# Values of both head pairs in one visit, left keys in four 64x64 tiles, and softmax sums half a quad later, in a fused soft-capped attention and max-of-two MoE kernel

## The chip, the cores and the metric

The kernel runs on one core of one Trainium2 chip. The metric is the device time of one execution in microseconds (us), and each kernel is given by the median of its runs. Engines: PE is TensorE's matmul, PEld its weight load, DVE VectorE, ACT ScalarE, POOL GpSimd, SP SyncE, whose queue issues most of the transfers ("SPq"). PSUM is the memory that this kernel's matmuls write and that DVE copies out ("evacuates") before it is written again; a "ones matmul" multiplies by a matrix of ones and so adds up the sums of the softmax. The "granted clock" is the share of TensorE's full clock that the profile shows.

## The reference, cut to what matters

```python
scores = q @ k^T / sqrt(64)                    # q, k, v: 8 batches x 12 heads x 448 x 64
scores = 30 * tanh(scores / 30)
attn   = exp(scores - max) / sum(...)          # softmax over 448 keys
x      = (attn @ v), heads side by side        # 3584 x 768
h1, h2 = x @ w1, x @ w2                        # 768 -> 1024
out    = maximum(h1, h2) @ w_out               # 1024 -> 768
```

The kernel writes max(h1, h2) as h2 + relu(h1 - h2). So it needs one product with `wd = w1 - w2`, a relu, and two products into the output, with `w_out` and with `wm = w2 @ w_out`, which is multiplied out once at the start.

## The kernel before: the parts that matter

Two heads make a pair, two pairs a quad; there are 24 quads. 448 keys are three blocks of 128 (`j` below) and 64 left over. A quad's left keys of both pairs lie in one tile, `expo[t, 2]`. Six pairs make one batch of tokens, three quads, and the MoE of a batch may start only when all its x is there.

```python
def values(t, ab):                       # one pair: 6 matmuls into 64 columns each, one full one for the left keys
    ps = pv_psum.tile([P, 512], f32, name="pv")
    for j in range(NJ):
        for h in range(2):
            nc.tensor.matmul(ps[HALF[h], :S], vp[g % 2][:, 2 * n + h, j, :], e_of(t, ab, j)[:, h, :], ...)
    nc.tensor.matmul(ps[:, :S], vl[g % 2][:, n, :], expo[t, 2][:, ab, :], start=False, stop=True)

# a quad's sums, on their way to x (17 of the 24 quads):
def total(t):    # ones matmuls on esum, copy to st, then: SP queue   sums <- st        (7 KB)
def invert(t):   # DVE reciprocal of sums, then:             SP queue   DRAM <- reciprocal
def spread(t):   #                                           SP queue   rec_b <- DRAM, to all partitions
def normalize(t):# POOL: x = u * rec_b, one multiply for each pair
# the other 7 quads ("CHIP") turn the sums with DVE transposes on the core, without a transfer
```

The main loop gives every engine its order. `F(n)` puts n MoE matmuls ("fill") into PE's order; `add` are the DVE additions that make the sums. Shortened:

```python
for t in range(3, NQ):
    if t % 3 == 0 and 3 < t < 13 or ...:  fill_q.append(moe(t // 3 - 1))   # a batch's MoE may start
    scores(t + 1, 0); ex(t, 3); F(2); add(t, 0, 1); F(6)
    if t in crosses: cross(crosses[t])      # SP queue: transposing DMA of a group of keys and queries
    spread(t - 2)                           # SP queue
    extra(i); F(5)                          # loads (SP queue) and casts (POOL) of groups to come
    scores(t + 1, 1); ex(t + 1, 0)
    keep(t, 0, values(t, 0))                # first visit, DVE copies the values to u
    F(4); add(t, 1, 0); F(6)
    normalize(t - 2)                        # POOL
    scores(t + 1, 2); ex(t + 1, 1)
    add(t, 0, 2); F(2); add(t, 1, 2); F(4); add(t, 1, 1); F(2)
    invert(t - 1)                           # DVE waits here for the sums of the quad before
    extra(i + 1); F(2)
    scores(t + 1, 3); ex(t + 1, 2)
    keep(t, 1, values(t, 1)); total(t)      # second visit, then at once the sums; sums <- st leaves here
    ...
```

## Time and profile before

| | before |
|---|---|
| median (runs) | 379.11 us (378.74 to 380.28) |
| span of the profiled execution, mean granted clock | 381.4 us, 0.977 |
| ACT busy; tanh and exp, the work that only ACT has | 281.6 us |
| ACT's idle gaps between its instructions (each about 0.2 us or more), added up from the timeline | 33.3 us, of which 18.2 in the first 75 us |
| length of an undisturbed quad | 11.8 us, ACT busy 11.7 of it |
| end of ACT's last exp to the end of the span (the "tail") | 63.9 us: ACT idle, PE busy 60.2, DVE 25.5 |

The way to read it: as long as ACT has work, a microsecond in which ACT stands is a microsecond of time, and one in which another engine stands costs nothing unless it makes ACT stand. The views that carry this are shown inside the prediction.

### The profile page before, as it was taken

What the parts mean: (1) busy time and instruction counts of PE and PEld (TensorE: products, weight loads), DVE (VectorE), ACT (ScalarE), POOL (GpSimd) and SP (SyncE); (2) the same over time, 40 slices, a digit from 0 to 9 for tenths busy, and PEclk for the clock granted to TensorE, in tenths of its full rate; (3) what the DMA queues carried; (4) which work ended last, traced back from release to release, by engine and by line L of the source; (5) the groups of instructions that cost most, each with busy time, mean ns of one, the idle gap of its engine ahead of it and who ended that gap; (6) DMA issues with size and microseconds to landing.
All of it is one profiled execution on the core that took longest, in us unless ns stands there. A gap on an engine that the chain in (4) does not pass through costs nothing.

```text
span 381.4 us, 6115 instructions
## 1 busy us (share of the span) xinstructions
PE 350.7 (92%) x2278; PEld 166.6 (44%) x2278; DVE 249.9 (66%) x413; ACT 281.6 (74%) x265; POOL 159.3 (42%) x193
## 2 busy tenths in 40 slices
PE   4799998999599988899999979999999899999996
PEld 2345443444144433244443434444443345555563
DVE  4237657868667768687877785787776878433521
ACT  4993778999869997699999996999999893000000
POOL 6644693703473238413582293427744232220000
PEclk9999999999789998899999998999999999999999
DMA  7999979573966599459994976788985032332022
GB/s 258 259 221 297 327 202 258 168 199 90 270 217 151 118 274 281 70 142 257 270 259 113 267 234 163 208 257 243 188 235 165 2 92 92 104 98 103 5 83 84
DMA packets 109523, 69.80 MB, mean 183 GB/s; under 512 B 64308, under 2 KB 104500, under 8 KB 109492
## 3 DMA queue, kind: packets, MB, share of 16 engines
q1 hardware_dynamic: 107540, 66.25, 62.3%
q0 software_dynamic: 1952, 3.15, 4.4%
q8 instruction: 18, 0.29, 0.3%
q14 instruction: 13, 0.11, 0.1%
HBM read 50.27 MB, written 11.13 MB: 161 GB/s over the span
## 4 chain that ended last, share of the span: by engine, by line
PE 45%; ACT 32%; DVE 7%; issue 4%; SPq 4%; DMA 3%; POOL 3%; POOLq 0%; DVEq 0%; ACTq 0%
ACT expo L306 15%; ACT tanh L299 14%; PE mm L455 11%; PE mm L470 10%; PE mm L467 7%; PE s L298 4%; PE pv L341 3%; PE mm L235 3%; ACT tanh L301 3%; DVE esum L329 2%; DMA qr<-in_q_dram 2%; PE pv L344 2%; POOL xT L418 1%; SPq L137 1%; SPq L271 1%
## 5 line engine op out<-in xcount | busy, mean ns | idle before, releaser
L299 ACT ACTIVATE tanh<-s 128x896 bf16<-128x896 f32 x144 | 124.2, 914 | 31.3 <-PE s L298 29.6
L306 ACT ACTIVATE expo<-tanh 128x1792 bf16<-128x1792 bf16 (+1 forms) x96 | 144.8, 1509 | 0.1
L470 PE MATMUL mm<-wo_sb,gT 128*128 128x384 bf16 x448 | 88.3, 332 | 0.0
L455 PE MATMUL mm<-xT,wd_sb 128*128 128x448 bf16 x384 | 82.1, 362 | 4.4 <-POOL xT L418 2.5
L418 POOL TENSOR_TENSOR xT<-u,rec_b 128x448 bf16<-128x448 f32 x34 | 41.8, 1248 | 96.1 <-DMA rec_b<-rec_d 75.0
L467 PE MATMUL mm<-wm_sb,xT 128*128 128x384 bf16 x336 | 69.9, 331 | 3.2 <-DVE osb L474 1.8
L470 PEld LDWEIGHTS <-gT 128*128 128x128 bf16 x448 | 43.4, 99 | 32.0 <-issue 5.8
L455 PEld LDWEIGHTS <-wd_sb 128*128 128x128 bf16 x384 | 37.1, 100 | 42.8 <-issue 10.8
L298 PE MATMUL s<-qkT 64*128 64x448 bf16 x288 | 46.4, 374 | 9.9 <-ACT tanh L299 4.8
L474 DVE COPY osb<-mm 128x384 f32<-128x384 f32 x56 | 30.9, 552 | 34.6 <-PE mm L470 34.4
L459 DVE TENSOR_SCALAR gT<-mm 128x448 bf16<-128x448 f32 x64 | 39.6, 619 | 18.5 <-PE mm L455 18.3
L350 DVE COPY u<-pv 128x448 f32<-128x448 f32 x38 | 23.3, 614 | 36.1 <-PE pv L344 34.3
L467 PEld LDWEIGHTS <-xT 128*128 128x128 bf16 x336 | 32.3, 99 | 24.7 <-issue 4.7
L329 DVE TENSOR_TENSOR esum<-esum,expo 128x896 bf16<-128x896 bf16 x42 | 38.9, 927 | 2.4
L159 POOL CAST vp<-vr 128x1152 bf16<-128x1152 f32 x14 | 16.8, 1203 | 46.4 <-DMA vr<-in_v_dram 30.8
L341 PE MATMUL pv<-expo,vp 128*64 128x448 bf16 x288 | 36.2, 359 | 0.0
L325 DVE TENSOR_TENSOR esum<-esum,expo 64x896 bf16<-64x896 bf16 x42 | 32.4, 771 | 0.8
L327 DVE TENSOR_TENSOR esum<-expo 128x896 bf16<-128x896 bf16 x42 | 31.8, 758 | 0.0
L298 PEld LDWEIGHTS <-qkT 64*128 64x128 bf16 x288 | 11.8, 95 | 44.2 <-issue 41.7
L301 ACT ACTIVATE tanh<-s 128x896 bf16<-128x896 f32 x24 | 22.0, 917 | 3.7 <-PE s L293 2.9
L341 PEld LDWEIGHTS <-vp 128*64 128x64 bf16 x288 | 13.1, 109 | 17.0 <-issue 11.8
L179 POOL CAST kqf<-kr 128x1152 bf16<-128x1152 f32 x14 | 17.3, 1237 | 5.5 <-DMA kr<-in_k_dram 5.2
(74 smaller groups left out, 268.7 us busy)
## 6 DMA issues: line engine op xcount, KB each, us to landing
kr<-in_k_dram SPq DMA_DIRECT2D x14, 576.0 KB, 5.6
qr<-in_q_dram SPq DMA_DIRECT2D x14, 576.0 KB, 7.0
vr<-in_v_dram SPq DMA_DIRECT2D x14, 576.0 KB, 4.4
out_dram<-osb SPq DMA_DIRECT2D x20, 384.0 KB, 3.6
rec_b<-rec_d SPq DMA_DIRECT2D x34, 224.0 KB, 3.6
out_dram<-osb SPq DMA_DIRECT2D x16, 192.0 KB, 3.1
osb<-in_moe_w_dram SPq DMA_DIRECT2D x4, 512.0 KB
gT<-in_moe_w_dram POOLq DMA_DIRECT2D x6, 256.0 KB, 11.9
```

What stands on the lines that cost most here:

```text
L298: nc.tensor.matmul(s[:, h, :S], k0[r, j * P : (j + 1) * P], qTn[r, :])
L299: nc.scalar.activation(tanh[t, p][:, 2 * m : 2 * m + 2, :], s[:, :, :S], AF.Tanh, scale=scale / cap)
L301: nc.scalar.activation(tanh[t, p][:, 0:2, :], s[:, :, :S], AF.Tanh, scale=scale / cap)
L306: nc.scalar.activation(expo[t, p], tanh[t, p][:, 0:n, :], AF.Exp, scale=float(cap))
L325: nc.vector.tensor_add(d, d, expo[t, 2][r, :, :])
L329: nc.vector.tensor_add(d, d, e_of(t, ab, 0 if ab else 2))
L341: nc.tensor.matmul(ps[HALF[h], :S], vp[g % 2][:, 2 * n + h, j, :], e_of(t, ab, j)[:, h, :], start=(j == 0), stop=False)
L418: nc.gpsimd.tensor_mul(x_of(t, ab), U[t][:, ab, :], rec[t][:, ab, :])
L455: nc.tensor.matmul(ps[:, :S], wd_sb[:, c, f * P : (f + 1) * P], x[:, c, cs], start=(c == 0), stop=(c == KC - 1))
L459: nc.vector.tensor_relu(g[:, f, cs], ps[:, :S])
L467: nc.tensor.matmul(ps[:, : DM // 2], x[:, c, ts], wm_sb[:, c, hs], start=(c == 0), stop=False)
L470: nc.tensor.matmul(ps[:, : DM // 2], g[:, f, ts], wo_sb[:, f, hs], start=False, stop=(f == FC - 1))
```

## The change

Its intent: fewer and wider DVE operations, no full matmul for 64 left keys, and no wait of PE for the additions behind the sums. The core of the diff:

```diff
-    def values(t, ab):          # per pair, one bank
+    def values(t):              # both pairs, one PSUM tile of two banks
+        ps = pv_psum.tile([P, 2, 512], f32, name="pv")
+        ...                     # 12 matmuls of 64 columns
+        for ab in range(2):
+            for h in range(2):
+                r = HALF[h ^ ab]
+                nc.tensor.matmul(ps[HALF[h], ab, :S], vl[g % 2][r, n, :], expo[t, 2][r, ab, :], start=False, stop=True)
+        nc.vector.tensor_copy(U[t], ps[:, :, :S])                  # one copy of 896 columns
@@ casts of the left keys and values (POOL): by odd and even pair, twice as many, with half the columns
-                eng.tensor_copy(vl[g % 2][r, n0:n1, r], l[r, n0:n1, :])
+                for n, to in left_rows(g, par):
+                    eng.tensor_copy(vl[g % 2][to, n, :], l[64 * par : 64 * par + 64, n, :])
@@ the 7 CHIP quads: both pairs in one chain (ones, transpose, reciprocal, transpose), multiplied on POOL
-        nc.vector.tensor_mul(x_of(t, 1), ps[:, :S], rb)
+        normalize(t)
@@ main loop
+        if t > 4 and t - 2 not in CHIP:
+            spread(t - 2)                      # now ahead of cross
         F(6)
         if t in crosses:
             cross(crosses[t])
-        if t > 4 and t - 2 not in CHIP:
-            spread(t - 2)
         ...
         extra(i)
         scores(t + 1, 1); ex(t + 1, 0)
-        keep(t, 0, values(t, 0))
+        sums_of(t - 1)                         # total(t - 1), or the chain of a CHIP quad
         ...
         invert(t - 1)                          # where it was
         ...
         scores(t + 1, 3); ex(t + 1, 2)
-        keep(t, 1, values(t, 1)); total(t)
+        values(t)
```

In one quad, 5 (`QUICK`), the chain still follows its values at once. A quarter of the diff rewrites the first three quads, the start, in the same style.

## The prediction

> **What bounds the kernel now.** I read the page's busy shares and slices first. PE is at 92% of the span and ACT at 74%, but ACT's work lies in the first 32 of 40 slices.
>
> ```profile
> PE 350.7 (92%) x2278; PEld 166.6 (44%) x2278; DVE 249.9 (66%) x413; ACT 281.6 (74%) x265; POOL 159.3 (42%) x193
> PE   4799998999599988899999979999999899999996
> ACT  4993778999869997699999996999999893000000
> PEclk9999999999789998899999998999999999999999
> ```
>
> So there are two phases. Up to about 317 us the attention's tanh and exp run on ACT, while PE fills its free time with a fixed count of MoE matmuls per quad (two head pairs). After that PE works alone, without a gap, through what is left. The tail's work is nearly fixed, so every microsecond by which ACT's phase ends sooner moves the end by one.
>
> Second, windows of single quads, then of the bad places (columns: PE, PEld, DVE, ACT, POOL busy, granted clock, DMA share, GB/s):
>
> ```profile
> 185.26:197.08 11.82, 11.44 (x75) 5.37 (x74) 8.27 (x13) 11.69 (x12) 11.31 (x14) 1.00 0.96 257
> 197.08:208.89 11.81, 11.81 (x72) 4.96 (x71) 9.96 (x16) 11.68 (x11) 4.40 (x5) 1.00 0.59 158
> 144.00:162.00 18.00, 16.18 (x84) 6.26 (x84) 13.25 (x16) 12.41 (x13) 12.38 (x15) 0.81 0.68 165
> 225.00:236.00 11.00, 8.30 (x45) 3.24 (x46) 7.97 (x9) 7.78 (x8) 6.94 (x8) 0.84 0.59 165
> ```
>
> A good quad takes 11.81 us with ACT busy 11.68 of it: ACT bounds it, and PE has little to spare (in the quad at 185 it waited for ACT's tanh 0.23 + 0.15 us). Nothing cheaper on PE or DVE shortens such a quad. In the bad windows ACT, PE and the clock all drop. Third, therefore, the waits of ACT and PE, and the timeline around one:
>
> ```profile
> ACT tanh L299 <- PE s L298: 29.6, 16, 5.6
> PE ss L362 <- DVE esum L329: 4.5, 2, 2.7
> ...
> 225.21 4.08 DVE L329 TENSOR_TENSOR esum<-esum,expo 128x896 bf16<-128x896 bf16 x1
> 225.51 2.21 POOL L418 TENSOR_TENSOR xT<-u,rec_b 128x448 bf16<-128x448 f32 x2
> 229.35 0.37 PE L362 MATMUL ss<-esum,ones 128*32 128x448 bf16 x2 [2.69 <-DVE esum L329]
> 231.68 1.73 ACT L299 ACTIVATE tanh<-s 128x896 bf16<-128x896 f32 x2 [2.54 <-PE s L298]
> 232.50 2.25 PE L470 MATMUL mm<-wo_sb,gT 128*128 128x384 bf16 x8
> ```
>
> This is one whole event. The last add of the quad's sums meets a POOL multiply and takes 4.08 us where it takes 0.62 alone. The ones matmul on those sums follows at once in PE's order, so PE stands for 2.69 us, the next scores come late, ACT stands for 2.54 us, and eight matmuls then take 2.25 us (1.30 at full clock).
>
> Adding ACT's single gaps in the timeline: 9.1 us at 34, 40, 44 and 55 us, plus 1.55 at 62 (the start); 4.70 at 108; 0.77 + 1.49 + 2.66 + 0.63 = 5.55 from 144 to 162; 2.54 + 0.65 = 3.19 at 231 and 235; 0.30 + 0.29 + 0.57 + 0.45 = 1.6 elsewhere. All but the start comes to 15.0 us.
>
> [...] two 64-row score matmuls of 448 columns take 0.24 us start to start, two 64-column value matmuls 0.23, and the full 128x128 one 0.20. That four 64x64 matmuls of this width pass together, no line shows. [...] the trace has 614 for the copy and 638 to 645 for the transposes. [...]
>
> **The change part by part.**
>
> (1) Left keys. Two 128x128 matmuls a quad (2 x 0.20 = 0.40 us) become four 64x64 ones into two banks. Side by side, my estimate from the 0.23 pairs is 0.25 us, so 0.15 saved. The two value visits become one: [...] That is some 0.3 us of PE a quad, 7 us over 24 quads. In ACT-bound quads it is only slack. It counts in the last two, PE-bound, quads: 0.5 us.
>
> (2) Wide DVE operations. Removed: 38 copies x 0.614 + 28 transposes x 0.642 + 14 reciprocals x 0.237 + 10 multiplies x 0.62 = 23.3 + 18.0 + 3.3 + 6.2 = 50.8 us. Added: 24 copies of 896 columns; [...] 1.08 each, 25.9 us; 14 transposes at 1.11, 15.5; 7 reciprocals at 0.26, 1.8; in all 43.2. DVE saves about 7.6 us of 250, nearly all off the path.
>
> (3) POOL takes the 10 multiplies that DVE did: 10 x 1.24 = 12.4 us. Each left cast is split by odd and even pair: two 64x192 pieces at about 0.34 become four at about 0.27 (from 0.18 fixed plus 0.83 ns a column), 0.4 us each for keys and values, over 16 groups 12 us. POOL goes from 159 to about 184 us, not a bound, but these sit in its order.
>
> (4) Sums half a quad later. The ones matmuls of quad t come after the second scores of t+1, some 5 us after the last add. A 4 us add ends before them. That removes the stalls at 152 and 226 us. With two reciprocal buffers, DVE's second transpose no longer waits for POOL (2.01 us at 141.7[...]).
>
> (5) Spread before cross. The broadcast of the reciprocals of quad 3 was issued at 95.50, behind a 3.28 us transposing DMA that held the queue, though they had been stored at 83.79; POOL's multiply therefore ran at 100.21 and PE's first MoE matmul of the second batch waited 1.60 us. Now it goes first. But quad 5 (done at once, "QUICK") has the chain copy 1.08, ones 0.4, transpose 1.11, reciprocal 0.25, transpose 1.11, POOL 2 x 1.24, some 6.5 us after its values, with about 3 us of other PE work over it. Before, the stall ended 6.7 us after the values. I keep a stall of 3 us, and take 1.5 us off.
>
> **The sum.** Start +0.5; stall at 100 to 108 -1.5; 144 to 162 -4.5 of 5.55; 231 to 235 -2.9 of 3.19; small gaps -1.0 of 1.6; last quads -0.5; new waits on the one two-bank value tile and on copies behind a long add +1.5. Together -8.4 us, or 370.7; I say 370.5.
>
> The start is my least sure term. In it PE is the bound, and 16 fewer fill matmuls (about 2.6 us) are asked of it before quad 3; but quad 0's sums now wait for the 1.08 us copy out of the same PSUM tile. Worse, the first three quads are normalized on POOL: the multiply of quad 1 stands ahead of four 2.13 us subtractions and the casts of group 3, and that of quad 2 behind them. I get quad 2 ready at about 60 to 63 us, against a MoE start that waited until 60.69 before.
>
> **The rivals.** (a) PE is the hidden bound everywhere, and its saving comes in full: 7 us more, 363 to 365. For it speaks PE's 11.81 of 11.81 in one quad; against it, ACT's 11.68 of the same quad and PE's waits for tanh. (b) The four small matmuls do not overlap: 4 x 0.19 = 0.76 us instead of 0.40, +0.36 a quad against a measured slack of 0.38. Quads would become PE-bound and much of the gain go, 373 to 377. [...] (c) POOL's larger load stretches DVE's adds more often (they already average 927, 771 and 758 ns against 0.62), or holds the first normalizations; stalls then come back at the PSUM evacuations or near 60 us: 374 to 379. POOL's idle 58% speaks against it, its place in the order for it. (d) The long value burst, [...] 3.3 us between scores, starves ACT: ACT then has 1.6 + 1.73 + 0.85 = 4.2 us queued, so no, by 0.7 us.
>
> **Range and chances.** The removed stalls are seen in the trace and the cure is direct, so slower is unlikely. The 2% line is 371.5, just above my figure. Range 364.5 to 376.5. Faster by over 2%: 0.57; within 2%: 0.39; slower: 0.04.
>
> **What would show it.** Right: no wait of the ones matmuls on the sums; quads still 11.8 us with ACT at 11.7; ACT's gaps after 100 us down from 15.0 to about 5; the four 64x64 matmuls in about 0.25 us; ACT's last exp 7 to 9 us sooner and the tail as long as before. Wrong: quads shorter than 11.8 us or PE the longer in them (then a); 0.6 us or more for the four (b); PE waiting for POOL's xT near 60 or 100 us longer than before, or for osb and gT copies (c); regular small ACT gaps after the values (d).

## The result, and the profile after

The changed kernel takes 408.27 us (median of 4 runs, 405.48 to 409.02) against 379.69 us of the kernel before in the same rounds. The ratio is 1.073, with a 95% interval from 1.067 to 1.080. (A ratio is the mean time of one kernel's fast runs over that of the other's of the same rounds, so it is not quite the ratio of the medians quoted.) It is clearly slower, by 28 us.

The page after, to be held against the page lines in the prediction (busy us, share, instructions; then 40 slices):

```profile
PE 351.5 (86%) x2326; PEld 166.9 (41%) x2326; DVE 250.2 (61%) x369; ACT 281.7 (69%) x265; POOL 188.9 (46%) x265
PE   3689996999599958599969997795999999999996
ACT  4795665999769986489967999983999996000000
PEclk9999997999989998799997999996999999999999
```

PE, DVE and ACT do as much work as before, to within 1 us. Only POOL does more, about as foreseen. What has changed is that PE and ACT now have dents together at slices 11, 15 to 17, 21 and 28, and that ACT's last quad comes 25 us later. The chain that ended last says of what kind the dents are. First before, then after:

```profile
PE 45%; ACT 32%; DVE 7%; issue 4%; SPq 4%; DMA 3%; POOL 3%; POOLq 0%; DVEq 0%; ACTq 0%
```

```profile
PE 38%; ACT 17%; POOL 12%; DMA 11%; SPq 9%; DVE 7%; issue 5%; POOLq 0%; DVEq 0%; ACTq 0%
```

Transfers and the SP queue went from 7% to 20% of the span, POOL from 3% to 12%. The path that sets the end now runs through a transfer again and again. The longest waits after (engine, line, what it waited for: us in all, times, the longest):

```profile
ACT tanh L311 <- PE s L310: 48.6, 20, 7.0
...
DVE rec_s L406 <- DMA sums<-st: 39.4, 11, 8.3
...
PE mm L445 <- POOL xT L428: 12.5, 8, 3.5
```

The second line is new. DVE's reciprocal of the sums waits for the transfer of the sums. What sat before that instruction, by the view of the tile `sums`, in before and after:

```profile
  DMA sums<-st: 1.3, 1
```

```profile
  DMA sums<-st: 39.4, 11
```

One of the eleven, in order of time. Before, around 127 us (start, duration, engine, line, operation):

```profile
126.87 0.61 DVE L366 COPY st<-ss 128x448 f32<-128x448 f32 x1
...
127.51 0.61 SPq L368 DMA_DIRECT2D sums<-st  x1
...
129.51 3.42 SPq L271 DMA_TRANSPOSE qkT<-kqf  x1
...
136.11 0.48 DVE L396 RECIPROCAL rec_s<-sums 32x56 f32<-32x56 f32 x1
```

The sums leave 0.03 us after their copy, and the reciprocal is asked for 8.6 us later: no wait. After, the same piece of another quad:

```profile
138.33 5.64 SPq L283 DMA_TRANSPOSE qkT<-kqf  x1
...
138.70 0.62 DVE L374 COPY st<-pv 128x448 f32<-128x448 f32 x1 [0.73 <-PE pv L372]
...
144.66 1.28 SPq L143 DMA_DIRECT2D kr<-in_k_dram  x2
...
147.33 0.62 SPq L376 DMA_DIRECT2D sums<-st  x1
...
151.34 0.49 DVE L406 RECIPROCAL rec_s<-sums 32x56 f32<-32x56 f32 x1 [8.33 <-DMA sums<-st]
151.76 1.01 DVE L366 COPY u<-pv 128x896 f32<-128x896 f32 x1
...
153.82 0.32 PE L457 MATMUL mm<-wm_sb,xT 128*128 128x384 bf16 x1 [4.31 <-DVE osb L464]
...
154.70 1.73 ACT L311 ACTIVATE tanh<-s 128x896 bf16<-128x896 f32 x2 [3.48 <-PE s L310]
```

The copy is done at 139.32, half a quad later than it would have been before. But it is now behind a transposing DMA and loads in the SP queue, so its transfer leaves only at 147.33, 8.0 us later, and its data is there at 151.3. DVE has stood 8.33 us by then, with the copy of the values and the evacuation of MoE results behind the reciprocal in its order. PE finds no free PSUM and stands 4.31 us, the next scores are late, ACT stands 3.48 us. The two windows on either side (us; PE, PEld, DVE, ACT, POOL busy; clock) show what it costs. The first quad is still the 11.8 us one, although DVE stands in it, and the bill comes in the second:

```profile
139.44:151.22 11.78, 9.16 (x61) 4.43 (x60) 3.05 (x5) 11.68 (x11) 2.22 (x2) 1.00 1.11 230
151.22:168.60 17.38, 11.14 (x65) 4.58 (x65) 14.91 (x16) 11.68 (x11) 11.64 (x17) 0.88 0.57 179
```

A second kind of dent lies where a batch's MoE starts. At 212 us, around the start of the fourth batch:

```profile
200.44 1.14 POOL L166 CAST vp<-vr 128x1152 bf16<-128x1152 f32 x1 [11.26 <-DMA vr<-in_v_dram]
201.53 1.95 POOL L171 CAST vl<-vr 64x64 bf16<-64x64 f32 x4
...
204.91 1.57 POOL L203 CAST kqf<-kr 64x128 bf16<-64x128 f32 x4
...
208.62 4.64 POOL L428 TENSOR_TENSOR xT<-u,rec_b 128x448 bf16<-128x448 f32 x4
...
212.22 0.53 PE L445 MATMUL mm<-xT,wd_sb 128*128 128x448 bf16 x1 [3.51 <-POOL xT L428]
...
214.80 1.73 ACT L311 ACTIVATE tanh<-s 128x896 bf16<-128x896 f32 x2 [4.50 <-PE s L310]
```

POOL's order has a value cast, whose load was late, then casts of a whole group, then four multiplies in a row that make the batch's last x. PE comes to that x at 208.7 and stands 3.51 us, ACT 4.50.

Adding up all of ACT's gaps of about 0.2 us or more gives 58.5 us after and 33.3 before. The difference is 25.2 us of the 25.8 by which the spans differ (407.2 and 381.4): 6.1 in the first 75 us, 19.1 later. So the whole loss is ACT standing, and three suspects are left: the round trip of the sums, x late at batch starts, and the start.

### The profile page after: what moved, and what is told of

It is laid out like the page before. It is cut to its first block, busy times and chain, and to the rows that moved or that the text cites. A ratio compares the mean times of both kernels' runs of the same rounds, so it can differ in the third digit from the quotient of the medians.

```text
span 407.2 us, 6229 instructions
## 1 busy us (share of the span) xinstructions
PE 351.5 (86%) x2326; PEld 166.9 (41%) x2326; DVE 250.2 (61%) x369; ACT 281.7 (69%) x265; POOL 188.9 (46%) x265
## 4 chain that ended last, share of the span: by engine, by line
PE 38%; ACT 17%; POOL 12%; DMA 11%; SPq 9%; DVE 7%; issue 5%; POOLq 0%; DVEq 0%; ACTq 0%
PE mm L445 13%; PE mm L460 9%; ACT expo L318 8%; ACT tanh L311 8%; PE mm L457 7%; POOL xT L428 4%; DMA sums<-st 4%; DMA qr<-in_q_dram 4%; PE s L310 4%; DMA vr<-in_v_dram 3%; PE pv L354 3%; SPq L283 3%; POOL kqf L190 3%; SPq L137 2%; POOL wd_sb L229 2%
## 5 line engine op out<-in xcount | busy, mean ns | idle before, releaser
L445 PE MATMUL mm<-xT,wd_sb 128*128 128x448 bf16 x384 | 90.4, 383 | 22.5 <-POOL xT L428 12.5
L428 POOL TENSOR_TENSOR xT<-u,rec_b 128x448 bf16<-128x448 f32 x48 | 59.8, 1269 | 64.0 <-DMA rec_b<-rec_d 46.8
L457 PE MATMUL mm<-wm_sb,xT 128*128 128x384 bf16 x336 | 68.5, 329 | 7.2 <-DVE osb L464 7.0
L445 PEld LDWEIGHTS <-wd_sb 128*128 128x128 bf16 x384 | 37.8, 103 | 68.1 <-issue 39.4
L166 POOL CAST vp<-vr 128x1152 bf16<-128x1152 f32 x14 | 16.5, 1181 | 85.1 <-DMA vr<-in_v_dram 41.3
L339 DVE TENSOR_TENSOR esum<-expo 128x896 bf16<-128x896 bf16 x42 | 37.4, 890 | 0.2
L337 DVE TENSOR_TENSOR esum<-esum,expo 64x896 bf16<-64x896 bf16 x42 | 36.6, 871 | 0.6
L366 DVE COPY u<-pv 128x896 f32<-128x896 f32 x24 | 25.6, 1067 | 14.4 <-PE pv L362 14.2
L341 DVE TENSOR_TENSOR esum<-esum,expo 128x896 bf16<-128x896 bf16 x42 | 32.2, 767 | 2.1
L354 PE MATMUL pv<-expo,vp 128*64 128x448 bf16 x288 | 31.8, 356 | 1.0 <-DVE wm_sb L580 1.0
L406 DVE RECIPROCAL rec_s<-sums 32x56 f32<-32x56 f32 x17 | 8.3, 488 | 39.4 <-DMA sums<-st 39.4
L203 POOL CAST kqf<-kr 64x128 bf16<-64x128 f32 (+1 forms) x56 | 21.6, 385 | 3.7 <-DMA kr<-in_k_dram 1.9
## 6 DMA issues: line engine op xcount, KB each, us to landing
out_dram<-osb SPq DMA_DIRECT2D x20, 384.0 KB, 3.6
```

The costliest lines, as they stand in the source:

```text
L337: nc.vector.tensor_add(d, d, expo[t, 2][r, :, :])
L339: nc.vector.tensor_add(d, e_of(t, ab, 1 if ab else 0), e_of(t, ab, 2 if ab else 1))
L341: nc.vector.tensor_add(d, d, e_of(t, ab, 0 if ab else 2))
L354: nc.tensor.matmul(ps[HALF[h], ab, :S], vp[g % 2][:, 2 * n + h, j, :], e_of(t, ab, j)[:, h, :], start=(j == 0), stop=False,)
L428: nc.gpsimd.tensor_mul(x_of(t, ab), U[t][:, ab, :], rec[t][:, ab, :])
L445: nc.tensor.matmul(ps[:, :S], wd_sb[:, c, f * P : (f + 1) * P], x[:, c, cs], start=(c == 0), stop=(c == KC - 1))
```

## The experiments

"Before" or "after" says which kernel was edited. Diffs are cut to the lines that matter. All gave right results. Ratios are to the kernel before in the same rounds (378.67 to 380.45 us).

**1. `sums_now`: after, with the sums taken at once after the values.**

```diff
-        sums_of(t - 1)                 # after scores(t + 1, 1)
         ...
         values(t)
         F(4)
+        sums_of(t)
```

> The changed kernel with the sums of every quad taken at once after its values, as before, all else kept. Theory 'round trip' (the sums' transfer leaves half a quad later, the reciprocal stands at its old place in DVE's order, and DVE stands there 39.4 us in all): DVE's wait for the sums falls below 4 us and the time to 390 to 397, the loss of the start staying. Rival 'start' (all of the loss comes from the first three quads and the batch starts they feed): 404 or more. Rival 'POOL' (the multiplies of the quads finished on the chip come late in POOL's order): also 390 to 397, so this run alone does not part it from 'round trip'.

Measured: 396.5 us (394.4 to 397.6), ratio 1.046 (1.041 to 1.052). DVE no longer waits for the sums at all, and 10 us come back by the ratios (1.073 to 1.046). But the sums' tile and the values' share the same two-bank buffers, so the ones matmuls come up against the copy of the values, 17 times:

```profile
PE pv L372 <- DVE u L366: 9.7, 17, 2.0
```

Most quads take 12.1 to 13.2 us instead of 11.8. So one visit per quad brings a reason to put the sums later, and putting them later has its own price.

**2. `invert_later`: after, with reciprocal, store and spread half a quad later as well.**

```diff
-            invert(t - 1)              # late in quad t
         ...
-            spread(t - 2)
+            invert(t - 2)              # at the start of the next quad
         F(6); cross(...); extra(i)
+            spread(t - 2)
```

> The sums stay half a quad late, but the reciprocal moves half a quad later too, to the start of the next quad, with the broadcast behind it. 'Round trip': DVE's wait for the sums falls below 5 us and the time to 391 to 398. 'POOL' (late x is the harm): x comes later still, so 405 to 412. 'Start': 404 or more.

Measured: 403.7 us, ratio 1.065 (1.058 to 1.071). This is a miss. DVE's wait fell only from 39.4 to 18.3 us, and PE's wait for x rose from 12.5 to 21.5. A later reciprocal takes half of DVE's wait away, but x comes later too; the edit also leaves the broadcast behind the transposing DMA and the loads. So the lateness itself seems to cost, and not only the place where DVE meets it.

**3. `sums_first`: after, with the transposing DMA and the loads behind the sums in the SP queue.**

```diff
-        cross(crosses[t]); extra(i)    # ahead of scores(t + 1, 1)
         scores(t + 1, 1); ex(t + 1, 0)
         sums_of(t - 1)
+        cross(crosses[t]); extra(i)
```

> Sums and reciprocal where the change has them, but in the DMA queue's order the transposing transfer and the loads of keys and queries now stand behind the sums' transfer instead of ahead of it. 'Round trip', with the queue's order as the main part of it: DVE's wait falls from 39.4 to under 15 us and the time to 394 to 401. If the distance alone is too short: the wait stays over 25 us and the time over 403. 'Start': 404 or more.

Measured: 399.4 us, ratio 1.054 (1.048 to 1.059). DVE's wait fell to 8.7 us (5 times), as expected, and 7 us of time came back. PE's wait for x was 16.1 us. The place in the queue is a part of the lateness: about half of what the half quad costs in time.

**4. `before_late`: before, with nothing but the sums half a quad later.**

```diff
         keep(t, 0, values(t, 0))
+        if t > 3 and t - 1 not in CHIP:
+            total(t - 1)
         ...
-            total(t)
```

> The kernel before with one thing changed: the ones matmuls, the copy and the transfer of the sums of the quads that go over DRAM come half a quad later; tiles, copies, casts and the start are the old ones. 'Round trip': DVE's wait for the sums goes from 1.3 to 15 to 40 us and the time from 379.5 to 386 to 396. 'Start' or 'POOL' alone: 377 to 383.

Measured: 395.3 us (392.4 to 396.5), ratio 1.043 (1.036 to 1.049), so 16 us are lost by this edit alone. Its wait before the reciprocal:

```profile
  DMA sums<-st: 26.7, 10
```

This is the decisive run: the kernel before, with narrow copies, the old start and old multiplies, loses over half of the change's loss when the sums alone are moved. The harm begins at the same place, DVE standing at the reciprocal, but part of it reaches PE by a path of the old kernel: at 144.57 us DVE had stood 6.49 us for the sums, and the ones matmuls of a CHIP quad waited 5.74 us for the DVE transpose behind it.

**5. `sums_quarter`: after, with the sums a quarter of a quad later only, ahead of spread, cross and loads in the queue.**

```diff
         ex(t, 3)
         F(2)
+        sums_of(t - 1)
         add(t, 0, 1)
         ...
-        sums_of(t - 1)
```

> The changed kernel with the sums at a third place: not half a quad after the values, and not at once, but after the first scores and two fill matmuls of the next quad, so that their transfer stands ahead of the broadcast, the transposing transfer and the loads in the queue, and PE no longer meets the 1.07 us copy out of the shared tile. 'Round trip' and the shared tile as its opposite cost: DVE's wait for the sums under 5 us, PE's waits for that copy (9.7 us in 17 places with the sums at once) under 2 us, time 385 to 391. If the remaining loss is the start and the batch starts: 394 to 399.

Measured: 391.5 us (390.1 to 393.8), ratio 1.034 (1.029 to 1.038), just outside the 385 to 391 expected. The wait before the reciprocal is gone, and so is most of PE's wait at the copy:

```profile
  DMA sums<-st: 0.2, 1
```

So 1.073 less 1.034, 3.95% of 380 us, is 15 us for the lateness of the sums; 4 gave 16 us. The two edits are not exact opposites (5 keeps a quarter of a quad of the lateness and also moves the chains of quads 4, 8 and 11, which 4 does not), so that they agree in sign and rough size is what counts. 12 to 13 us stay unexplained. All further edits of the changed kernel except 7 start from this one.

**6. `quick_three`: `sums_quarter` with three quads whose chain follows the values at once.**

```diff
-    QUICK = (5,)
+    QUICK = (5, 8, 11)
```

> The run before it, with quads 8 and 11 also finished at once (as quad 5 is), because the MoE of the next batch needs them first. Theory 'late x': PE's waits for x at the batch starts fall by 3 to 6 us and the time by 3 to 6 us against that run. If the batch starts wait for POOL's order rather than for the sums: within 1.5 us of it.

Measured: 390.5 us, ratio 1.032 (1.027 to 1.037). That is 0.9 us where 3 to 6 were expected, a miss. The quad at the fourth batch's start went from 15.1 to 13.1 us and PE's wait for x from 12.8 to 9.9, but the chain right after the values made its own quads (8 and 11) about 1 us longer.

**7. `start_dve`: after, with the first three quads multiplied on DVE.**

```diff
-            nc.gpsimd.tensor_mul(x_of(t, ab), U[t][:, ab, :], rec[t][:, ab, :])
+            eng = nc.vector if t < NS else nc.gpsimd
+            eng.tensor_mul(x_of(t, ab), U[t][:, ab, :], rec[t][:, ab, :])
```

> The changed kernel, but the first three quads are normalized on DVE instead of POOL; all else, the late sums too, kept. Theory 'start' as I predicted it (POOL's multiplies stand in the way of the subtractions and of the first MoE matmuls): ACT's gaps before 75 us fall from 24 to about 19 us and the time from 408 to 402 to 405. If the start is lost elsewhere (the order of DVE's subtraction, the split casts): 406 to 410.

Measured: 409.8 us, ratio 1.081 (1.077 to 1.085; one slow run left out). It cures nothing. My reason for the start, the multiplies standing among POOL's subtractions, falls.

**8. `before_spread`: before, with the broadcast ahead of the transposing DMA.**

```diff
+            spread(t - 2)
         F(6)
         cross(crosses[t])
-            spread(t - 2)
```

> The kernel before with only the broadcast of the reciprocals moved ahead of the transposing transfer, as in the change. My prediction gave this part 1.5 us: 376.5 to 378.5 against 378.7 if so, with the 1.60 us wait of PE at 101 us gone. If it only moves the wait to the later transposing transfer: 378 to 381.

Measured: 376.9 us (375.9 to 378.1), ratio 0.995 (0.991 to 0.999). The stall at 101 us is gone (that quad went from 16.6 to 12.0 us), as step (5) of the prediction said. But part of it comes back: at 152 us PE waits 2.90 us for x, and that quad takes 17.7 us instead of 15.1. POOL's multiply is behind group casts there.

**9. `left_only`: before, with nothing but the left keys in 64x64 tiles and the split casts.**

```diff
-        nc.tensor.matmul(ps[:, :S], vl[g % 2][:, n, :], expo[t, 2][:, ab, :], start=False, stop=True)
+        for h in range(2):
+            r = HALF[h ^ ab]
+            nc.tensor.matmul(ps[HALF[h], :S], vl[g % 2][r, n, :], expo[t, 2][r, ab, :], start=False, stop=True)
```

> The kernel before with only the layout of the left keys and values changed: the split casts, and two 64x64 matmuls per pair instead of one 128x128; values still in two visits, sums at the old time. If the split casts (POOL's 12 us more, two more DVE casts at the start) hurt by themselves: 381.5 to 386 against 379.4. If they lie in POOL's idle time: 377.5 to 381.

Measured: 380.5 us (one slow run left out), ratio 1.002 (0.995 to 1.008). By itself this part shows neither a cost nor a gain, to within 3 us. (Here each pair has its own visit, so two tiles at a time and not four.)

**10. `quarter_start`: `sums_quarter`, with the DVE subtraction of the start behind the third quad's chain.**

```diff
-            subtract(5)
         run(chip(t), 4)
         if t == 2:
+            subtract(5)
```

> The run with the sums a quarter of a quad late (391.5), with DVE's subtraction of the start moved behind the transposes of quad 2: it took 3.18 us beside POOL's subtraction and PE waited 2.4 us for the copy behind it. If that wait is the start's loss: PE's 2.4 us wait at 62 us gone, time 387.5 to 390. If PE then waits for POOL's x instead: 390 to 393.

Measured: 391.3 us, ratio 1.032 (1.028 to 1.036): nothing. PE's wait at the first MoE matmuls for `wm` fell from 2.39 to 0.81 us, and it then waited 2.11 and 0.56 us for POOL's x (0.64 and 0.74 in `sums_quarter`) instead.

**11 and 12. `quarter_norm` and `before_norm`: the multiplies of POOL ahead of the casts, in every quad.** The first edits `sums_quarter`, the second `before_spread`.

```diff
+            normalize(t - 2)
         extra(i)                       # loads and casts
         ...
-            normalize(t - 2)
```

> The run with the sums a quarter late, with POOL's multiplies of two quads ago ahead of the casts of the same quad. Theory 'POOL's order' (the batch starts wait because the multiplies stand behind casts that wait for loads): PE's waits for x, 12.8 us in all, fall to 6 to 9, the 7.62 us gap of ACT at 167 us falls below 4 and the time to 384 to 388. If the sums themselves come too late: within 2 us of 391.5.

> The kernel before with the broadcast first (376.9), and the same reordering of POOL's multiplies. 'POOL's order': the 5.18 us gap of ACT at 158 us goes and the time falls to 371 to 374.5. Otherwise 375.5 to 378.

Measured: 390.0 us (1.029) and 380.1 us (1.001), so by the ratios `sums_quarter` gained 1.6 us and `before_spread` lost 2.3: both misses (384 to 388 and 371 to 374.5 were expected of the theory). In `quarter_norm` PE's wait for x fell from 12.8 to 4.4 us, yet the multiplies now wait for their broadcast with the casts behind them, the casts feed the transposing DMA, and PE waits for that (3.1 us, 2 times, in `sums_quarter`):

```profile
PE s L310 <- DMA qkT<-kqf: 8.8, 4, 3.5
```

One wait took the place of another: POOL's order has no place that is good in every quad.

**13. `quarter_oldstart`: `sums_quarter` with the first three quads pair by pair, as before, but in the two banks of the one shared tile.**

```diff
-    values(0); F(8); run(chip(0), 4)
+    run(chip0(0, 0), 8)                # sums in bank 0, values in bank 1 of one tile
+    run(chip0(0, 1), 6)
```

> The run with the sums a quarter late (391.5), with the first three quads done as before: pair by pair, sums and values in the two banks of one tile, multiplied on DVE from PSUM, and the old fill counts. If the wide one-visit chain is the start's loss: quads 1 to 3 take 58 to 59 us again instead of 60.1 and the time is 387 to 389. If the split casts or the transfers are: within 1.5 us of 391.5.

Measured: 397.5 us, ratio 1.048 (1.044 to 1.051), a miss and worse by 5 us. The second and third intervals between quads' tanh took 24.3 and 16.4 us (20.5 and 14.8 in `sums_quarter`): sums and values share one tile, and in it the values' matmuls waited for DVE's transpose of the sums (4.9 us, 6 times), which ties the two chains to each other. It could not restore the old start, so it does not say what the new one costs.

**14. `quarter_half`: `sums_quarter` with every second multiply of the CHIP quads on DVE.**

```diff
+            eng = nc.vector if ab and t in CHIP else nc.gpsimd
```

> The run with the sums a quarter late, with the second half of each chip quad multiplied on DVE, as before, instead of POOL. Theory 'POOL takes both halves': PE's wait at the batch start of quad 6 (2.38 + 1.12 us) falls by about 1.2 us, POOL frees up by 8 us, time 388 to 390. If POOL's second multiply is hidden: 390.5 to 392.5.

Measured: 390.9 us, ratio 1.032 (1.028 to 1.036). The quad of the second batch's start went from 16.5 to 15.6 us; the time is the same within the error.

**15. `before_nine`: `before_spread` with the multiply ahead of the casts in quad 9 alone** (where 8 had shown the new wait).

```diff
-        if t > 4 and t - 2 not in CHIP:
+        if t > 4 and t - 2 not in CHIP and t != 9:
             normalize(t - 2)
...
+        if t == 9:
+            normalize(t - 2)
         extra(i)
```

> The kernel before with the broadcast first (376.9), and the multiplies of quad 7 alone ahead of the casts in POOL's order, at quad 9, where MoE batch 2 waited for them (5.18 us of ACT's time). If that one place is the cause and nothing else moves: 371.5 to 374. If the delayed casts give it back as they did with all quads reordered: 376 to 380.

Measured with five rounds: 374.5 us (372.5 to 377.7), ratio 0.989 (0.984 to 0.993). It beats both kernels, by 4.3 us against before: a gain clear of the noise, though below 2%. The quad in question takes 12.5 us instead of 17.7.

**16. `quarter_all`: `sums_quarter` with 13, 14 and 15 together.**

> The sums a quarter late, the old start, half of the chip's multiplies on DVE, and quad 7's multiplies ahead of the casts, together: the one-visit values with the 64x64 tiles and the two-bank tile stay. If these three account for the rest of the loss: 376 to 382, the level of before. If one visit and the shared tile cost by themselves: 384 or more.

Measured: 392.9 us, ratio 1.038 (1.033 to 1.042). Of the outcomes it is the one that says that one visit and the shared tile cost by themselves, but since 13 is in it, it says no more than 13 does.

**17. `quarter_hold`: `sums_quarter` with the second batch's MoE let in half a quad later.**

```diff
-        if t % 3 == 0 and 3 < t < 13 or ...:
+        if t % 3 == 0 and 6 < t < 13 or ...:
             fill_q.append(moe(t // 3 - 1))
         ...
         scores(t + 1, 1); ex(t + 1, 0)
+        if t == 6:
+            fill_q.append(moe(1))
```

> The run with the sums a quarter late (391.5), with MoE batch 1 put into the fill queue half a quad later, behind the second scores of quad 6. 'Late x': PE's wait for x there (2.38 + 1.12 us) and ACT's gap of 4.21 us at 111 us go, quad 6 falls from 16.5 to 12 to 13 us, and the 13 fill matmuls come back in the tail (+2.2 us): 389 to 390.5. If x is not there half a quad later either: 391 to 394.

Measured: 383.7 us (381.7 to 385.8), ratio 1.011 (1.005 to 1.017). That is 8.6 us by the ratios (2.27% of 380) where 1 to 2.5 were expected, a miss in size. The group of the first MoE product (busy us, mean ns; idle before it and what ended it), in before, `before_late`, `sums_quarter` and `quarter_hold`:

```profile
L455 PE MATMUL mm<-xT,wd_sb 128*128 128x448 bf16 x384 | 82.1, 362 | 4.4 <-POOL xT L418 2.5 <-DVE wd_sb L217 1.7 <-POOL xT L435 0.2
```

```profile
L455 PE MATMUL mm<-xT,wd_sb 128*128 128x448 bf16 x384 | 84.5, 366 | 11.2 <-POOL xT L418 4.0 <-DVE gT L459 2.9 <-DVE osb L474 2.4
```

```profile
L445 PE MATMUL mm<-xT,wd_sb 128*128 128x448 bf16 x384 | 86.4, 369 | 15.7 <-POOL xT L428 12.8 <-DVE wm_sb L252 2.4 <-DVE gT L449 0.5
```

```profile
L445 PE MATMUL mm<-xT,wd_sb 128*128 128x448 bf16 x384 | 85.0, 363 | 8.8 <-POOL xT L428 3.2 <-DVE gT L449 2.5 <-DVE wm_sb L252 2.4
```

The fill is one sequence. A batch that starts half a quad later is half a quad behind at its end too, so the next starts shift with it. The quads of the second, third and fourth start went from 16.5, 19.4 and 15.1 us to 13.1, 12.3 and 11.8; the quad after the second start went the other way, from 13.1 to 15.2. Late sums alone hardly make PE wait for POOL's x (4.0 us against 2.5); the changed kernel, its sums early again, does (12.8). The run shows that 8.6 us go when the batch starts are held by half a quad. It also lays the fill matmuls differently around them, which the run does not separate from x. And the hold was not tried on before, where a batch start stalls too (its quad at 101 us takes 16.6 us), so it is not shown that the change caused all of these 8.6 us.

**18. `before_fill`: `before_nine` with 16 fill matmuls fewer in the first quad.**

```diff
-    run(chip(0, 0), 8)
-    run(chip(0, 1), 6)
+    run(chip(0, 0), 4)
+    run(chip(0, 1), 2)
```

> The best kernel so far (before, broadcast first, quad 7's multiplies ahead of the casts: 374.5), with 16 fewer fill matmuls asked for in the first quad, as many as the queue later runs dry by. My prediction's step: PE is the bound there, so ACT's gap of 5.78 us at 35 us falls by 2 to 2.6 us and the time to 371.9 to 372.7. If the PSUM evacuations or the loads bound the start: 374 to 375.5.

Measured with five rounds: 374.4 us (373.4 to 375.6), ratio 0.987 (0.982 to 0.992), the same as `before_nine`. ACT's gap at 33 us fell from 5.78 to 4.12 us and later ones grew: work moved out of one stall at the start lands in the next.

**All of them in one table.** Spans and gaps are of one profiled execution each (that of before took 383.1 us, 4 above its median), so 2 us more or less in a gap may be chance; the wait for x is that of PE's first MoE product for POOL's multiplies.

| kernel | ratio | span | ACT's gaps: first 75 us, later | DVE's wait for the sums | PE's wait for x | span less gaps |
|---|---|---|---|---|---|---|
| before | 1 | 381.4 | 18.2 + 15.1 | 1.3 | 2.7 | 348.1 |
| after | 1.073 | 407.2 | 24.3 + 34.2 | 39.4 | 12.5 | 348.7 |
| before_late | 1.043 | 392.5 | 19.0 + 24.4 | 26.7 | 4.0 | 349.1 |
| invert_later | 1.065 | 403.0 | 21.9 + 33.5 | 18.3 | 21.5 | 347.6 |
| sums_first | 1.054 | 396.9 | 23.6 + 24.8 | 8.7 | 16.1 | 348.5 |
| sums_now | 1.046 | 395.8 | 20.3 + 27.1 | 0 | 7.3 | 348.4 |
| sums_quarter | 1.034 | 389.7 | 21.1 + 20.8 | 0.2 | 12.8 | 347.8 |
| quarter_hold | 1.011 | 384.0 | 22.7 + 11.7 | 0.9 | 3.2 | 349.6 |
| before_spread | 0.995 | 376.0 | 18.4 + 9.0 | 1.3 | 3.5 | 348.6 |
| before_nine | 0.989 | 372.3 | 18.4 + 5.4 | 1.3 | 1.1 | 348.5 |

The last column stays between 347.6 and 349.6. ACT's work and PE's tail are nearly the same everywhere, and a kernel's time is decided by how long ACT stands. The ledger of the loss, by the ratios on 380 us: after 27.8 us; 15.0 of it ends with the sums early (5), 8.6 more with the second batch held (17, with the reserve said there), and 4.2 stay. In the traces `quarter_hold` is 2.6 us longer than before: gaps of the start 4.5 more, later ones 3.4 fewer, the rest 1.5 more. So in these two executions what stays lies mostly in the start.

## Why the prediction was wrong

It said 370.5 us; 408.3 were measured. The step that failed is (4), "Sums half a quad later".

**(4), the failed step.** It says of the ones matmuls "A 4 us add ends before them. That removes the stalls at 152 and 226 us", and booked -4.5 and -2.9 us. The first half is right: no ones matmul waits for the sums' additions after. But it followed the sums only up to PE. Behind the ones matmuls there are a copy, a transfer in the SP queue, a reciprocal in DVE's order, a store and a broadcast, and the reciprocal was left at its old place. Before, the sums had 8.6 us from their issue to the reciprocal (shown at 127.51). Half a quad, 5.9 us, taken from that leaves 2.7 us, less than the 4.0 us that the transfer shown was under way (147.33 to 151.34), even without the up to 8 us of other transfers put ahead: 39.4 us of waits on DVE, and through DVE's evacuations PE and ACT. The runs put -15 us (5) and +16 us (4) on this; the step has the wrong sign. Both numbers that it needed, the distance from issue to reciprocal and the transposing DMA's duration, stood in the trace of before. Its second point, the transpose that waited for POOL, is seen in the trace of before: the wait at 141.70 is 2.01 us, the osb copy starts at 143.45 and PE stands 1.75 us for it. The granted clock was 0.66 from 144 to 149 us; what lowered it is not shown.

**(3), POOL.** It says that POOL's 184 us are "not a bound, but these sit in its order", and booked nothing. The busy time was right (188.9: multiplies +13.1 us for 12.4, small casts of the main groups 26.8 to 41.8 us, so +15.0 for 12). Two things were under-read. One is the size of a cast: 0.34 us for a 64x192 piece is what casts of the start took (343 to 344 ns; the estimate of 0.18 us and 0.83 ns a column fits them and the starting casts of 1152 and 1344 columns, 1143 and 1303 ns), but in the main groups they already took 462 to 497 ns before. The other is their place: in the batch start shown, two groups of split casts take 1.95 and 1.57 us and stand ahead of four multiplies. Rival (c) named it, with 374 to 379 us. The longer additions that it speaks of are in the trace of before: 67 of the 126 had no POOL instruction beside them and took 0.60 to 0.63 us, and the 50 that had one for over half of their time took 0.60 to 4.08, 1.11 on average. As to the order, holding a batch start gave 8.6 us in (17). The split casts alone do no harm (9); with the long chain of a quad, the multiplies of both pairs together and x wanted at once they probably stand in the way. How these share the 8.6 us was not separated.

**(5), spread ahead.** Right in mechanism: alone on before (8) the stall at 101 us goes and the ratio is 0.995, -2 us where -1.5 was booked. The "kept" stall of 3 us for the quick quad was there too: the quad takes 17.0 us, as long as before (16.6), so the changed kernel got nothing of the 1.5 us.

**(1), left keys and one visit.** Right. The visit after, and one of the two visits before (start, duration):

```profile
179.91 1.32 PE L354 MATMUL pv<-expo,vp 128*64 128x448 bf16 x12
181.16 0.38 PE L362 MATMUL pv<-expo,vl 64*64 64x448 bf16 x4
```

```profile
189.87 0.76 PE L341 MATMUL pv<-expo,vp 128*64 128x448 bf16 x6
190.56 0.36 PE L344 MATMUL pv<-expo,vl 128*128 128x448 bf16 x1
```

The four small matmuls overlap: 0.32 us to the next start, where four in turn were put at 0.76. So rival (b) is out. Twelve take 1.25 us to the next start and four 0.32 start to start, 1.57 us; before, the visit shown took 0.69 and 0.29 to the next start, where ones matmuls follow, and a quad's first visit, with fill behind it, 0.69 and 0.20: 1.78 to 1.87 for the two. So 0.21 to 0.30 us a quad are saved on PE, 0.3 were said, and as said they are slack: the undisturbed quad is 11.8 us in both kernels. (What the 0.3 has beyond the 0.15 was an estimate from the score visits of before: a 384-column matmul at full clock was followed by the next after 0.16 us, by a score after 0.26.) Rival (a) is out with that, and (d) too, as such quads show no regular gap: around the visit shown the scores start 3.48 us apart (179.43 and 182.91), and no gap of ACT there is over 0.15 us.

**(2), wide DVE operations.** The durations put down for them were estimates. Copies took 1.07 us for 1.08, transposes 1.11 for 1.11, reciprocals 0.32 for 0.26; the operations named add up to 43.5 us after 50.7. For the copies the trace of before gives nearly the same: 552 ns for 384 columns and 614 for 448, 0.97 ns a column, so by estimate 1.05 us for 896. But DVE's busy time is 250.2 us after 249.9. Other operations took more: the sums' additions 106.2 us for 103.1, a subtraction at the start 3.18 us for 1.22; the rest was not followed up, as it was off the path either way.

**The start.** +0.5 was booked, as the least sure term. ACT's gaps of the first 75 us are 20.3 to 24.3 us in the versions of the changed kernel that keep its start and are in the table, and 18.2 to 19.0 in those of before: about 1 to 6 us. Outside the table `before_norm`, with the old start, shows 20.5, so a part of this is chance. Three tries to find the cause missed (7, 10, 13), and it stays open.

**Slips that bear on nothing.** ACT's work lies in the first 34 of 40 slices, not 32. The start's gaps at 34, 40, 44 and 55 us are 5.55, 1.96, 1.06 and 2.06, which is 10.6 and not 9.1; no term was booked from it. The 1.30 us for eight matmuls "at full clock" are start to start (193.88 to 195.18 us, clock 1.00); by that measure those at 232.50 took 2.10, at a clock of 0.62.

What allowed the confidence: the range left only 4% for slower, since "the removed stalls are seen in the trace and the cure is direct". It was direct for the engine that stood, and was not followed to the next one that needs the same data.

## What to carry to other kernels

When a producer is moved later, follow its data to the last consumer, with the slack of each hop read from the trace (here 8.6 us from the issue of the sums to their reciprocal), and look at what else lies in the queue that carries it; an engine that meets the late data in its order holds up what stands behind (8.33 us of DVE here). Keep the ledger of the bounding engine's gaps for each version: here span less gaps was some 348.5 us in all, so a cure that only moves a wait (6, 11, 12, 18) is seen at once. The gain that was to be had, 1.1% in `before_nine`, came from two reorderings in the old kernel and not from fewer instructions.

## What the traces show of single operations

- The issue of one transposing DMA held the SP queue for 3.1 to 5.6 us (14 of them after, median 3.6), against a median of 5.8 us to landing, and a 7 KB transfer that was ready at 139.32 us left at 147.33.
- Four 64x64 matmuls of 448 columns into two PSUM banks took 0.32 us start to start (181.16 to 181.48, after), and a pair of 64-column ones 0.21 (twelve in 1.25).
- On POOL a 64x192 cast took 462 to 497 ns on average before, and the two that replace it, 64x128 and 64x64, 378 to 406 and 342 to 364 ns after: here a third of the columns took three quarters of the time.
